# Stationary v for three segments, shared diagonal scores, early split transposes of x, gate operations on GpSimd, and a newly searched order, in a kernel of segmented attention beside a spectral layer

## The chip, the cores and the metric

The kernel runs on one core of one Trainium2 chip. The metric is device time in microseconds (us), the median of several runs. A run also has a span (what the profile covers, 1.7 to 2.1 us shorter than the time of the same run) and a mean granted clock of TensorE (PE below), 1.0 at full speed. ACT is ScalarE, DVE is VectorE, POOL is GpSimd, SP is the engine that issues most transfers.

A ratio below is the mean time of one kernel's fast runs over the mean of the other's fast runs of the same rounds, so it is not quite the ratio of the medians quoted beside it. The interval is the 95% interval of that ratio. "Same" means within 2%. The calls ran on different chips of the same kind, so kernels of different calls are best compared by their ratios to the kernel before of the same call.

## The reference, cut to what matters

Tokens: 2048, width 640, 32 heads of width 20, in 4 segments of 512. Each segment has causal softmax attention inside itself and reads a linear memory that the segments before it have left. A spectral layer runs on the same input, and a gate per token mixes the two.

```python
for s in range(N):                                   # N = 4 segments of L = 512
    logits = einsum('bhqd,bhkd->bhqk', qs, ks) * scale + mask
    p = softmax(logits);  a_dot = einsum('bhqk,bhkd->bhqd', p, vs)
    num = einsum('bhld,bhde->bhle', phi(qs), M)      # phi(t) = t+1 if t > 0 else exp(t)
    den = einsum('bhld,bhd->bhl', phi(qs), z)[..., None] + 1e-06
    outs.append(g * num / den + (1 - g) * a_dot)
    M, z = M + phi(ks)^T vs, z + sum(phi(ks))
a = o @ wo
b = irfft2(rfft2(x) * (w_r + 1j * w_i))
return gate * a + (1 - gate) * b                     # gate = sigmoid(x . gate_w), per token
```

## The kernel before

The kernel is one flat list of instructions: each engine executes its own in a fixed order that a search has found. Heads are handled in 8 groups of 4 per segment. A score unit fills four PSUM banks by matmuls on row tiles, one exponential of up to 128x2048 moves it to SBUF, POOL zeroes the part above the diagonal, and then the product with v (PV) follows. PV keeps the exponentials stationary and streams 21 columns of v (20 and a column of ones, which gives the softmax denominator), 40 matmuls a group:

```python
def pv_group(self, s, g):                            # (cut)
    for i in range(4):                               # block of 128 queries
        for hh in range(4):
            for jj in range(i + 1):                  # block of 128 keys
                # out 128 x 21, stationary: exponentials 128 x 128, moving: v
                return (self.ps(bank, i * 88 + hh * VW, [1, DH + 1]),
                        self.ex.ap(self.exo(s, g) + hh * 1280 + JOFF[jj] + (i - jj) * P, [1, P]),
                        va.ap(jj * H * VW + (4 * g + hh) * VW, [1, DH + 1]), jj == 0, jj == i, {})
    # DVE: denominators times gate, reciprocal, product -> on (128 tokens per partition block)
    ...
    # later: store of on to DRAM, transposed load of it as oT, output projection with wo
```

The order of the loads at the start is one transposed load of three 128-column blocks of x, then one of two.

The softmax here doesn't subtract the row's maximum and nothing guards it: scores larger than these inputs give would overflow.

## Time and profile before

| what | before |
|---|---|
| median time, 4 runs | 246.55 us (246.41 to 250.81) |
| profiled span, granted clock | 244.2 us, 1.0 |
| PE busy, and span less PE busy | 233.1 us, 11.1 us |
| ACT, DVE, POOL busy | 201.6, 198.8, 132.2 us |
| start of the first score exponential on ACT | 13.32 us |
| moved by DMA | 36.71 MB |

The lines behind these numbers are in the prediction. "Span less PE busy" is the time in which PE does nothing.

### The profile page before, as it was taken

What the parts mean: (1) busy time and instruction counts of PE and PEld (TensorE: products, weight loads), DVE (VectorE), ACT (ScalarE), POOL (GpSimd) and SP (SyncE); (2) the same over time, 40 slices, a digit from 0 to 9 for tenths busy, and PEclk for the clock granted to TensorE, in tenths of its full rate; (3) what the DMA queues carried; (4) which work ended last, traced back from release to release, by engine and by line L of the source; (5) the groups of instructions that cost most, each with busy time, mean ns of one, the idle gap of its engine ahead of it and who ended that gap; (6) DMA issues with size and microseconds to landing.
All of it is one profiled execution on the core that took longest, in us unless ns stands there. A gap on an engine that the chain in (4) does not pass through costs nothing.

```text
span 244.2 us, 8905 instructions
## 1 busy us (share of the span) xinstructions
PE 233.1 (95%) x3702; PEld 139.8 (57%) x3702; DVE 198.8 (81%) x534; ACT 201.6 (83%) x204; POOL 132.2 (54%) x200
## 2 busy tenths in 40 slices
PE   7999999999999999999978999999899999999994
PEld 2344575557556457645644475645555667667683
DVE  1489997988999898979999999989999975643643
ACT  2088889999998998999987998888899878798820
POOL 8421861362648484455876385646567656407610
PEclk9999999999999999999999999999999999999999
DMA  7998866696493656756442546313442969586224
GB/s 185 328 358 231 218 172 169 205 182 172 138 192 92 168 128 150 226 164 200 109 104 71 144 137 182 94 59 111 118 100 71 203 144 97 79 123 116 77 62 131
DMA packets 55880, 36.71 MB, mean 150 GB/s; under 512 B 31792, under 2 KB 52128, under 8 KB 55840
## 3 DMA queue, kind: packets, MB, share of 16 engines
q1 hardware_dynamic: 54144, 35.32, 58.4%
q10 hardware_dynamic: 1696, 0.82, 1.2%
q8 instruction: 29, 0.48, 0.8%
q14 instruction: 11, 0.09, 0.1%
HBM read 19.86 MB, written 9.71 MB: 121 GB/s over the span
## 4 chain that ended last, share of the span: by engine, by line
PE 72%; DVE 16%; DMA 5%; ACT 4%; issue 2%; SPq 0%; DVEq 0%
PE psum L498 64%; PE psum L496 8%; DVE Pt L1287 4%; ACT ex L1137 3%; DMA xT<-in_A_x_dram 2%; DMA oT<-o_scr 2%; DVE Cp L509 2%; DVE Yt L1292 1%; DVE qu L509 1%; ACT et L1010 1%; DVE va L1045 1%; DVE Bt L509 1%; DVE on L1172 1%; DVE on L1177 0%; DVE phk L1021 0%
## 5 line engine op out<-in xcount | busy, mean ns | idle before, releaser
L1137 ACT ACTIVATE ex<-psum 128x2048 bf16<-128x2048 f32 x80 | 150.3, 1878 | 15.8 <-PE psum L498 14.8
L1140 POOL TENSOR_SCALAR_AFFINE_SELECT ex<-ex 128x512 bf16<-128x512 bf16 x128 | 81.0, 653 | 70.5 <-ACT ex L1137 66.7
L498 PEld LDWEIGHTS psum<-va,ex 128*128 128x128 bf16 x1280 | 39.0, 96 | 5.8 <-issue 1.3
L498 PE MATMUL psum<-va,ex 128*128 128x21 bf16 x1280 | 41.1, 172 | 0.1
L498 PE MATMUL psum<-xT,wk 128*128 128x512 bf16 (+1 forms) x140 | 33.3, 380 | 0.6 <-DMA xT<-in_A_x_dram 0.6
L498 PE MATMUL psum<-xT,wq 128*128 128x512 bf16 (+1 forms) x135 | 32.2, 380 | 1.2 <-DVE Bt L509 1.2
L498 PE MATMUL psum<-qp,kp 20*128 20x384 bf16 (+3 forms) x512 | 31.7, 301 | 0.7 <-ACT ex L1137 0.2
L498 PE MATMUL psum<-wv,xT 128*128 128x500 bf16 (+1 forms) x160 | 31.9, 300 | 0.2
L1287 DVE TENSOR_TENSOR Pt<-psum,Wt 128x642 bf16<-128x642 f32 x32 | 25.4, 822 | 0.8 <-PE psum L498 0.5
L496 PE MATMUL psum<-wo,oT 128*32 128x320 bf16 x480 | 23.0, 300 | 0.2 <-issue 0.2
L498 PEld LDWEIGHTS psum<-qp,kp 20*128 20x128 bf16 x512 | 9.0, 92 | 18.3 <-ACT ex L1137 9.6
L509 DVE CAST ot<-psum 128x320 bf16<-128x320 f32 x21 | 9.9, 489 | 11.6 <-PE psum L496 8.4
L498 PEld LDWEIGHTS psum<-wv,xT 128*128 128x128 bf16 x160 | 13.3, 97 | 10.0 <-DVE Ac L509 0.8
L498 PE MATMUL psum<-big,Ac 128*128 128x321 bf16 (+2 forms) x96 | 17.9, 256 | 0.8 <-DVE Cp L509 0.4
L1045 DVE TENSOR_TENSOR va<-psum,ebx 128x500 bf16<-128x500 f32 (+1 forms) x32 | 15.2, 484 | 3.5 <-PE psum L498 2.8
L498 PE MATMUL psum<-tt,Yt 128*128 128x256 bf16 (+1 forms) x96 | 17.0, 274 | 0.4 <-DVE qu L509 0.2
L1292 POOL TENSOR_TENSOR Yt<-Pt 128x321 bf16<-128x321 bf16 x18 | 13.4, 757 | 7.2 <-DVE Pt L1287 4.6
L509 DVE CAST qu<-psum 128x512 bf16<-128x512 f32 x20 | 13.6, 686 | 3.4 <-PE psum L498 3.2
L1333 DVE TENSOR_TENSOR G<-eo,psum 128x320 bf16<-128x320 f32 x32 | 14.9, 479 | 1.7 <-PE psum L496 0.9
L498 PEld LDWEIGHTS psum<-xT,wk 128*128 128x128 bf16 (+1 forms) x140 | 9.9, 97 | 10.9 <-issue 2.3
L1177 POOL TENSOR_TENSOR on<-on,mem 128x320 bf16<-128x320 bf16 x16 | 12.8, 806 | 5.8 <-DVE on L1172 5.8
L1172 DVE TENSOR_TENSOR on<-psum,rs 128x320 bf16<-128x320 f32 x32 | 15.3, 481 | 0.6
(85 smaller groups left out, 379.9 us busy)
## 6 DMA issues: line engine op xcount, KB each, us to landing
tt<-tab_tt SPq DMA_DIRECT2D x16, 256.0 KB, 3.3
xsb<-in_A_x_dram SPq DMA_DIRECT2D x8, 320.0 KB
kp<-k_scr SPq DMA_DIRECT2D x28, 80.0 KB
qp<-q_scr SPq DMA_DIRECT2D x28, 80.0 KB
o_scr<-on SPq DMA_DIRECT2D x12, 160.0 KB
out_dram<-ot SPq DMA_DIRECT2D x12, 160.0 KB
q_scr<-qu SPq DMA_DIRECT2D x6, 256.0 KB
k_scr<-qu SPq DMA_DIRECT2D x6, 256.0 KB, 3.9
```

Of the source, the lines that this page charges most:

```text
L496: h = e.matmul(dst, wt, r_, start=st, stop=sp_, **{**kw, "tile_position": (0, q), "skip_group_check": True})
L498: h = e.matmul(o_, l_, r_, start=st, stop=sp_, **kw)
L509: alts["dve"] = (lambda e: e.tensor_copy(dst(), src()), 67 + 1.04 * n, 68.0)
L1010: self.one("act", lambda e: e.activation(et.ap(0, [1, L]), qsl(), ACT.Exp), L, [qb], [b("et", pi_)], late, name="phi_exp")
L1045: self.one("dve", lambda e: e.tensor_tensor(va.ap(i * H * VW + h0 * VW, [VW, nh], [1, DH]), self.ps(bank, 0, [DH, nh], [1, DH]), self.ebx. ...
L1137: self.one("act", lambda e: e.activation(dst(), src(), ACT.Exp, scale=SC), 4 * width, [bank], [self.exb(s, g, j) for g, j in outs], prio - ...
L1140: self.one("pool", lambda e, g=g, j=j: e.affine_select(self.ex.ap(self.exo(s, g) + JOFF[j], [1280, 4], [1, P]), self.ex.ap(self.exo(s, g) ...
L1172: self.one("dve", lambda e, rs=rs, bank=bank, g=g: e.tensor_tensor(on.ap(80 * g, [D, 4], [DH, 4], [1, DH]), self.ps(bank, 0, [88, 4], [VW, ...
L1177: self.either(lambda e, g=g: e.tensor_tensor(on.ap(80 * g, [D, 4], [1, 80]), on.ap(80 * g, [D, 4], [1, 80]), self.mem.ap(80 * g, [D, 4], [ ...
L1287: self.one("dve", lambda e, ri=ri, Pt=Pt, Wt=Wt, bank=bank: e.tensor_tensor(Pt.ap(ri * 322, [644, 2], [1, KD]), self.ps(bank, 0, [0, 2], [ ...
L1292: fn = lambda e, r=r, a0=a0, a1=a1, op=op, Pt=Pt, Yt=Yt: e.tensor_tensor(Yt.ap(r * 322, [1, KD]), Pt.ap(a0 * 322, [1, KD]), Pt.ap(a1 * 322 ...
L1333: self.one("dve", lambda e, q=q, n2=n2, bank=bank, eo=eo: e.tensor_tensor(self.G.ap(n2 * D + 639 * q, [1 - 2 * q, 320]), eo.ap(q, [1, 320] ...
```

## The change

The intent: PE leads, so let it do PV with v stationary (32 columns of v on one of four column tiles, the exponentials streaming), which needs 24 packed matmuls a group for 40 small ones; compute no score twice on the diagonal, so that exponentials get narrower; start earlier; take work off DVE. The core of the diff (cut: tables, buffers, the new order, the layout of tokens that goes with it):

```diff
-        self.xt_load(0, 0.0, 0, 3)
-        self.xt_load(0, 0.01, 3, 2)
+        self.xt_load(0, 0.0, 0, 1)
+        self.xt_load(0, 0.01, 1, 2)
+        self.xt_load(0, 0.02, 3, 2)
 ...
             for g in (2 * pr, 2 * pr + 1):
-                self.pv_group(s, g)
+                if s < 3:
+                    self.pv_flipped(s, g)
+                else:
+                    self.pv_group(s, g)
 ...
+    def pv_flipped(self, s, g):
+        for n_, (jj, o, n, q0) in enumerate(VPIECES):   # 512, 384, 192, 64, 64, 64 columns
+            for hh in range(4):
+                    return (self.ps(bank, q0, [1, n], p0=32 * hh, np_=32), va.ap(jj * H * VW + (4 * g + hh) * VW, [1, 32]),
+                            self.ex.ap(self.exo(s, g) + hh * 1280 + o, [1, n]), n_ == 0, n_ == 5,
+                            {"tile_position": (0, 32 * hh), "skip_group_check": True})
+        # eviction by ACT or DVE, store of the unnormalised result
+    def denominators(self, s):
+        # load of the denominators, reciprocal, times gate, store as r
 ...
+            # output stage: load r and the stored result, oU = oU * r, oU = oU + mT (memory part), then wo
 ...
-                    items.append((th, n / 4.0))      # scores: row tiles 32 x 128
+                    items.append((th, n / 8.0))      # scores: tiles 32 x 64
```

## The prediction

> **What bounds the kernel now.** I read the page first, then the stage table, the chain of waits and the timelines of three short stretches. From the page:
>
> ```profile
> PE 233.1 (95%) x3702; PEld 139.8 (57%) x3702; DVE 198.8 (81%) x534; ACT 201.6 (83%) x204; POOL 132.2 (54%) x200
> ...
> PE 72%; DVE 16%; DMA 5%; ACT 4%; issue 2%; SPq 0%; DVEq 0%
> ...
> L1137 ACT ACTIVATE ex<-psum 128x2048 bf16<-128x2048 f32 x80 | 150.3, 1878 | 15.8 <-PE psum L498 14.8
> L1140 POOL TENSOR_SCALAR_AFFINE_SELECT ex<-ex 128x512 bf16<-128x512 bf16 x128 | 81.0, 653 | 70.5 <-ACT ex L1137 66.7
> L498 PEld LDWEIGHTS psum<-va,ex 128*128 128x128 bf16 x1280 | 39.0, 96 | 5.8 <-issue 1.3
> L498 PE MATMUL psum<-va,ex 128*128 128x21 bf16 x1280 | 41.1, 172 | 0.1
> L1172 DVE TENSOR_TENSOR on<-psum,rs 128x320 bf16<-128x320 f32 x32 | 15.3, 481 | 0.6
> ```
>
> The third to seventh lines give count, busy time and mean duration, then the idle time before. The reader should see three engines close together: PE leads and carries 72% of the chain, ACT and DVE are both above 80%, and GpSimd has 112 us of idle time, of which 66.7 us is waiting for an exponential. PE's 95% contains pipeline latency (a 21-column matmul is shown as 172 ns), so I count its work from the program. All full-array streams together (projections, v, scores, memory, the spectral half and the output projections) are about 392,000 columns. The timeline of the last projections shows 28 matmuls of 320 columns on 32-column tiles taking 1.12 us, and 4 taking 0.31 us, so (1.12-0.31)/24 = 33.8 ns each, or 0.42 ns per column after packing four side by side. That makes 392,000 x 0.417 = 163 us. The price of a PV group and of a change of array mode is in this stretch of PE's timeline (start, length, what):
>
> ```profile
> 206.02 0.40 PE L498 MATMUL psum<-qp,kp 20*128 20x512 bf16 x4
> 206.35 2.17 PE L498 MATMUL psum<-va,ex 128*128 128x21 bf16 x80
> 208.45 0.40 PE L498 MATMUL psum<-qp,kp 20*128 20x256 bf16 x8
> ```
>
> Two PV groups, 80 matmuls, take (2.17-0.15)/80 = 25.3 ns each, so 1.01 us a group and 32 us for 32 groups. The score unit needs 512 x 0.417 = 213 ns of stream but 0.33 us pass until the next work: about 0.1 us is a change of mode. 80 units with a change on either side are about 16 us. With some 4 us of small gaps between matmuls PE's real work is 163+32+16+4 = 215 us, of a window of 234 us between the first useful matmul (7.4 us) and the last (about 241). The roughly 19 us left are stalls. Where they lie shows in the stage table and at the start:
>
> ```profile
> 110.00:130.00 20.00, 18.16 (x265) 10.82 (x261) 19.70 (x46) 17.87 (x20) 14.30 (x22) 1.00 0.50 135
> 150.00:170.00 20.00, 19.98 (x253) 10.98 (x253) 17.91 (x47) 17.58 (x15) 12.36 (x21) 1.00 0.33 91
> 170.00:190.00 20.00, 18.86 (x281) 11.20 (x279) 19.21 (x63) 18.04 (x17) 13.85 (x19) 1.00 0.39 101
> ...
> 1.27 5.96 DMA xT<-in_A_x_dram
> 7.36 19.51 PE psum L498 x179
> ```
>
> Columns of the first three: PE, PEld, DVE, ACT, POOL busy, clock, DMA. At 110 to 130 and 170 to 190 DVE is full and PE is not; at 150 to 170 PE is full. The last two lines, from the chain in order of time, say that PE cannot start before the transposed load of three blocks of x has landed.
>
> [...]units of eight row-tiled matmuls (384 and 128 columns) last as long as units of four with 512, 0.40 us[...].
>
> **The change part by part.**
>
> *PV with v stationary, segments 0 to 2.* 24 of 32 groups replace 40 matmuls of 25.3 ns by 24 packed ones, six pieces of 512, 384, 192, 64, 64 and 64 columns, together 1280: 1280 x 0.417 = 0.53 us plus small gaps, 0.545 us. The saving is 24 x (1.01-0.545) = 11.2 us of PE. In return it is another array mode: one more change per group, 24 x 0.1 = 2.4 us, and the odd v tiles, whose rows are now permuted by column tiles, up to 16 x 0.2 = 3 us if the order does not bunch them. Net PE about -7.
>
> *Shared diagonal scores.* Per pair of groups the five units have widths 512, 512, 512, 512, 256 where they had five times 512. PE: 16 x 256 x 0.417 = -1.7 us. ACT: 598 ns for 512 and 1878 for 2048 elements make 0.833 ns per element and a fixed 171, so 1024 elements take 1.02 us. Segments 0 to 2: 12 x (1.88-1.02) = -10.2; segment 3 has its exponentials split: four pairs each lose 1.88 and gain two of 0.60, and two units each split at +0.17, so 4 x (-0.68+0.34) = -1.4. Sum -11.6 us of ACT. GpSimd pays: four masks a group become seven, three of 512 elements and four of 256. With 634 ns as typical for 512 and an estimated 430 for 256, a group goes from 2.54 to 3.62 us, 32 groups +35 us.
>
> *Normalisation moved.* DVE loses, per flipped group, 168+244+481 = 0.89 us (the denominators, the reciprocal, the multiplication): 24 x 0.89 = -21.4. It is replaced by 24 evictions of 512 columns (598 ns on ACT, 686 on DVE: +15.4 over the two), 15 products of 512 and 8 sums of 640 bf16 elements on DVE or GpSimd (0.45 and 0.55 us on DVE, so 11.2 there, or some 27 on GpSimd), three reciprocals of 128 columns (the 16 and 32 column ones take 244 and 335 ns, so an estimated 0.9 each) with their products, about 4. The memory sums of segments 1 and 2 (16 at 0.43 to 0.81) go. DVE and ACT together: -11.6-21.4+15.4+4+1.4 (eight more gate exponentials) +6 = about -6 us, of 400.
>
> *Round trip.* The unnormalised result goes out in 12 stores of 256 KB and back in 15 loads of 128 KB, in place of 4 of the 12 stores of 160 KB and 4 of the 12 transposed loads. The DMA share is 0.3 to 0.5 where most of it happens; segment 2's falls into 190 to 210, at 0.81. Weights, tables and padded q and k come in fewer, larger transfers[...].
>
> *Start.* The transposed load of three blocks becomes one block and then two; six warm-up matmuls of 0.43 us go. PE should begin real work 1 to 2 us earlier; I take 1.5.
>
> *Gate operations on GpSimd, new order.* Some 1 to 3 us of DVE; the order cannot be costed by hand.
>
> Sum: PE -7-1.7 = about -9, start -1.5, so 244.2-10.5 = 233.7 us of span if stalls stay at 19 us. DVE was the cause in the two stretches above and loses about a tenth of its work there; I take 2 us of stalls back. 231.7 of span, plus the 2.3 us by which the timed median exceeds the span now (246.55-244.2): 234.
>
> **The rivals.** First, GpSimd becomes the bound. 132+35, less 8 for memory sums, plus some of the moved work, is 165 to 180 us, or 70 to 77%. For it: seven dependent masks stand before each PV group[...]. Against it: 70.5 us of idle time ahead of the masks and no 20 us stretch above 72%. It would return half of the gain: 239 to 242. Second, the small tiles cost a floor of 25 ns each. Score matmuls go from 512 to about 1280, PV from 960 to 576; at 25 ns the scores alone would cost about 15 us more and the kernel would end near 246. The eight-tile units speak against it, but no instruction here is as small as 64 columns on 64-column tiles. Third, ACT stays the bound: it does 14 to 15 us of exponentials in each 20 us now, and if it takes most evictions its sum stays near 197 to 201. Then only 3 to 5 us come: 241. Fourth, the round trip of segment 2 delays the outputs at 205 to 215, where the chain now already holds a 5.2 us transposed load: +2 to 4 us. In the other direction, the three engines all fall and the order has been searched anew with other transfer costs: down to 226.
>
> **Range and chances.** 234 us, with 227 to 241.5 holding it 8 times in 10. Faster by over 2% means under 241.6: 0.88. Within 2%, which needs the tile floor or GpSimd to take nearly everything: 0.10. Slower: 0.02, as no added work is on the engine that leads the chain.
>
> **What would show it.** Right: a flipped group of 24 matmuls within 0.55 to 0.65 us on PE's timeline; exponentials at 128x1024 near 1.02 us and ACT's exponential sum near 139; GpSimd at 165 to 180 us with PE's waits for masks still under 5 us; first projection before 6.5 us; DVE below its 19 us of 20 at 110 to 130. Wrong: packed matmuls of 64 columns spaced at 25 ns, PE's loads waiting many us for masks or for ACT, DVE's two-input operations lengthened against the durations above, or a new wait for the returned result between 200 and 220 us.

The sum comes to about -9-1.5 = -10.5, so 233.7 us of span, 231.7 with 2 us of stalls back, and 234 of time. Some of its figures are estimates, and this is what the traces show beside them:

- Its 0.417 ns per column is an estimate; measured are 0.42, both as 33.8 x 4/320 and as three matmuls of 512 columns in 0.65 us (kernel before, 62.18 to 62.83). The 0.15 us taken off two PV groups is about the shown length of one 21-column matmul less its spacing (172 less 25 ns).
- The 0.1 us for a change of mode is an estimate from score units: the next work starts 0.32 to 0.33 us after such a unit does (206.02 to 206.35), where 512 columns on the whole array take 0.215. That the change of mode is the cause was not shown.
- The floor of 25 ns in the second rival is a supposition: the 25.3 ns of the 21-column matmuls carried over to other shapes.
- The estimated 430 ns of a mask of 256 elements were 481 in the changed kernel (128x256, mean of 128). "Some 27" us on GpSimd is an estimate too: a sum of 640 takes 1.39 us there in both kernels, a product of 512 by r 1.16 in the changed one.

## The result, and the profile after

The changed kernel took 247.12 us (246.77 to 247.59, 4 runs) against 246.55 (246.41 to 250.81) of the same rounds. The ratio of the fast runs is 1.0026 (1.0003 to 1.0049): the same within 2%, where 234 was predicted, and outside the predicted range. Executions over 1.5% slower than the fastest of the same kernel are left out of the means. The granted clock was 0.985 to 0.993 in all four runs of the changed kernel.

The page of the changed kernel, in the form of the one before (busy us, share and count of each engine; the chain that ended last by engine; masks; exponentials):

```profile
PE 229.2 (94%) x4347; PEld 141.3 (58%) x4361; DVE 197.3 (81%) x481; ACT 199.3 (81%) x241; POOL 166.5 (68%) x297
...
PE 59%; DVE 14%; DMA 10%; ACT 9%; SPq 3%; issue 2%; ACTq 0%; DVEq 0%
...
L1284 POOL TENSOR_SCALAR_AFFINE_SELECT ex<-ex 128x256 bf16<-128x256 bf16 (+2 forms) x224 | 122.1, 567 | 41.1 <-ACT ex L1263 37.7
...
L1263 ACT ACTIVATE ex<-psum 128x2048 bf16<-128x2048 f32 (+4 forms) x92 | 138.7, 1508 | 13.9 <-PE psum L514 12.0
```

The work moved as planned. Exponentials are 138.7 us where 150.3 were, masks 122.1 where 81.0 were, and POOL stands at 166.5. The DMA engines moved 42.17 MB where they moved 36.71. PE is busy for 3.9 us less, but the span is not shorter: span less PE busy is 244.7-229.2 = 15.5 us, 4.4 more than before. And PE's 229.2 us hold a stretch at half clock, which the stage table shows (columns: PE, PEld, DVE, ACT, POOL busy, granted clock, DMA share, GB/s):

```profile
206.00:208.00 2.00, 1.58 (x58) 1.26 (x42) 1.97 (x5) 1.69 (x2) 1.60 (x2) 1.00 1.11 119
208.00:210.00 2.00, 0.96 (x16) 0.63 (x20) 1.93 (x6) 0.36 (x1) 0.28 (x2) 0.58 0.19 39
210.00:212.00 2.00, 2.00 (x56) 1.00 (x48) 1.11 (x3) 1.11 (x3) 0.80 (x2) 0.50 0.61 163
212.00:214.00 2.00, 2.00 (x40) 0.93 (x36) 0.75 (x2) 0.52 (x1) 1.46 (x3) 0.50 1.34 134
214.00:216.00 2.00, 2.00 (x44) 1.19 (x48) 0.53 (x2) 1.76 (x2) 0.00 (x0) 0.71 0.48 91
```

The lost clock adds up to 2 x (0.42+0.50+0.50+0.29) = 3.4 us, that is 6.8 us at half clock. So PE's work at full clock fell by up to 3.9+3.4 = 7.3 us (a little less, since PE stood idle in a part of that stretch). The reader should see that a busy PE here is partly a slow PE: at 210 to 214 it shows 2.00 of 2.00.

What stopped PE just before is in the timelines of PE, DVE and POOL (start, length, what; in brackets the idle time ahead and what ended it):

```profile
209.04 0.46 PE L514 MATMUL psum<-G,fbg 128*32 128x320 bf16 x4 [1.46 <-DVE on L1325]
```

```profile
206.98 1.60 DVE L1534 TENSOR_TENSOR oU<-oU,mT 128x640 bf16<-128x640 bf16 x1
208.51 0.48 DVE L1325 TENSOR_TENSOR on<-psum,rs 128x320 bf16<-128x320 f32 x1
```

```profile
206.84 1.39 POOL L1534 TENSOR_TENSOR oU<-oU,mT 128x640 bf16<-128x640 bf16 x1 [0.40 <-DVE rs L1320]
```

PE waited for the normalised product of a PV group (L1325), and DVE had put a sum of the new output stage (L1534) ahead of it, which lasted 1.60 us beside the same kind of sum on POOL (the seven such sums of DVE in this trace take 0.43 us at the least and 0.48 in the median). In two later traces it took 1.08 us beside POOL's sum (the late sum moved, at 207.16, and both losses mended, at 205.54), and in all three it ended 0.34 to 0.35 us after POOL's did; what ties the two, no record names. That is one loss of the changed kernel. The other is at the start. The chain there and PE's timeline:

```profile
4.45 6.75 DMA xT<-in_A_x_dram
```

```profile
5.70 1.05 PE L514 MATMUL psum<-xT,wq 128*32 128x512 bf16 x8
...
11.25 0.40 PE L514 MATMUL psum<-xT,wq 128*32 128x512 bf16 x4 [1.70 <-DMA xT<-in_A_x_dram]
```

PE begins at 5.70 instead of 7.36, as predicted, but the third piece of x takes 6.75 us to land, PE stands still for 1.70 us, and the first score exponential starts at 14.83 us, 1.5 later than before.

### The profile page after: what moved, and what is told of

Read it like the earlier page. It is cut to its first block, busy times and chain, and to the rows that moved or that the text cites. A ratio compares the mean times of both kernels' runs of the same rounds, so it can differ in the third digit from the quotient of the medians.

```text
span 244.7 us, 10242 instructions
## 1 busy us (share of the span) xinstructions
PE 229.2 (94%) x4347; PEld 141.3 (58%) x4361; DVE 197.3 (81%) x481; ACT 199.3 (81%) x241; POOL 166.5 (68%) x297
## 2 busy tenths in 40 slices
DMA packets 58928, 42.17 MB, mean 172 GB/s; under 512 B 30020, under 2 KB 55172, under 8 KB 58884
## 4 chain that ended last, share of the span: by engine, by line
PE 59%; DVE 14%; DMA 10%; ACT 9%; SPq 3%; issue 2%; ACTq 0%; DVEq 0%
PE psum L514 53%; PE psum L512 7%; ACT ex L1263 6%; DMA xT<-in_A_x_dram 3%; DMA pkn<-phk 2%; SPq L548 2%; DMA r<-r_scr 2%; DVE Pt L1439 2%; DMA qk_scr<-qu 2%; DMA r_scr<-rc 2%; SPq L546 1%; DVE G L1485 1%; DVE phk L1085 1%; DVE oU L1526 1%; ACT et L1072 1%
## 5 line engine op out<-in xcount | busy, mean ns | idle before, releaser
L1284 POOL TENSOR_SCALAR_AFFINE_SELECT ex<-ex 128x256 bf16<-128x256 bf16 (+2 forms) x224 | 122.1, 567 | 41.1 <-ACT ex L1263 37.7
L1263 ACT ACTIVATE ex<-psum 128x2048 bf16<-128x2048 f32 (+4 forms) x92 | 138.7, 1508 | 13.9 <-PE psum L514 12.0
L514 PE MATMUL psum<-qkp 20*64 20x64 bf16 (+5 forms) x1280 | 32.7, 272 | 2.2 <-ACT ex L1263 1.7
L514 PE MATMUL psum<-xT,wk 128*128 128x256 bf16 (+1 forms) x280 | 34.1, 276 | 0.2 <-issue 0.2
L514 PE MATMUL psum<-wv,xT 128*32 128x321 bf16 (+3 forms) x400 | 30.1, 301 | 0.6 <-DVE va L1115 0.3
L512 PE MATMUL psum<-wo,oU 128*32 128x320 bf16 x480 | 23.5, 319 | 0.0
L514 PE MATMUL psum<-big,Ac 128*128 128x160 bf16 (+2 forms) x96 | 18.1, 258 | 0.7 <-DVE Pt L1439 0.3
L514 PE MATMUL psum<-big,Cp 128*128 128x321 bf16 (+1 forms) x96 | 18.0, 302 | 0.2 <-DVE G L1485 0.2
L514 PE MATMUL psum<-ex,va 128*32 128x64 bf16 (+3 forms) x576 | 17.4, 256 | 0.7 <-DVE dn L1152 0.3
L514 PEld LDWEIGHTS psum<-ex,va 128*32 128x32 bf16 x576 | 11.1, 96 | 9.7 <-POOL ex L1284 3.4
L1072 ACT ACTIVATE et<-qu 128x512 bf16<-128x512 bf16 x25 | 15.6, 629 | 0.1
```

What stands on the lines that cost most here:

```text
L512: h = e.matmul(dst, wt, r_, start=st, stop=sp_, **{**kw, "tile_position": (0, q), "skip_group_check": True})
L514: h = e.matmul(o_, l_, r_, start=st, stop=sp_, **kw)
L1072: self.one("act", lambda e: e.activation(et.ap(0, [1, L]), qsl(), ACT.Exp), L, [qb], [b("et", pi_)], late, name="phi_exp")
L1263: self.one("act", lambda e, d=d, q=q: e.activation(self.ex.ap(*d), self.ps(bank, *q), ACT.Exp, scale=SC), n, [bank], [self.exb(s, 2 * pr + ...
L1284: self.one("pool", lambda e: e.affine_select(self.ex.ap(e0 + d0, [1280, 4], [1, n], np_=np_), self.ex.ap(e0 + s0, [1280, 4], [1, n], np_=np_),
```

## The experiments

Sixteen kernels ran. Each call had its own runs of the kernel before (medians 246.49 to 246.72), except where another is named. "Mended" is the kernel of the fourth run, the changed kernel with both losses above taken out.

### First question: are the start and the late sum what ate the gain?

The theory: the two losses above cost about 4 us together, and the rest of the predicted saving was never there. The rival: the saving is there and some larger thing eats it.

**Start.** The second half of wk (560 KB) and one 320 KB block of x, which the ACT queue issued beside the transposed loads, go to the SP queue behind the third of them. In the list of the order:

```diff
-  ... 35 (wk, second half, ACT queue) ... 45 (x block, ACT queue) ... 30 (third transposed load) ...
+  ... 30 (third transposed load), 34 (wk, SP queue), 44 (x block, SP queue) ...
```

> Changed kernel, only the place of two early loads altered: 560 KB of wk and 320 KB of x go out on the sync queue behind the third transposed piece of x instead of on ACT's queue beside it. Theory (the loads on ACT's queue share the 16 DMA engines with the third transposed piece, which then lands at 11.25 us and holds PE): the third piece lands before 9.6 us, the first score exponential starts near 13 us instead of 14.8, and the time falls by 1.5 to 2 us. Rival (the split into three pieces itself is slow): it still lands near 11 us and the time does not change.

Measured: 243.75 us, ratio 0.9854 (0.978 to 0.9928), result right. Its two runs at full clock took 242.5 and 242.1, two at clock 0.986 took 245.0 and 247.4 (the last counts as slow). That is more than the 1.5 to 2 us expected. The third piece of x is no longer waited for on PE's timeline, and the first exponential starts at 13.70:

```profile
9.63 0.39 PE L514 MATMUL psum<-xT,wq 128*32 128x512 bf16 x4
...
11.99 0.27 PE L514 MATMUL psum<-xT,wk 128*128 128x256 bf16 x1 [0.45 <-DMA wk<-in_A_wk_dram]
```

**The split itself.** The transposed load goes back to three blocks and two, the ACT loads stay.

```diff
-        self.xt_load(0, 0.0, 0, 1)
-        self.xt_load(0, 0.01, 1, 2)
-        self.xt_load(0, 0.02, 3, 2)
+        self.xt_load(0, 0.0, 0, 3)
+        self.xt_load(0, 0.01, 3, 2)
```

> Changed kernel with the two-piece split of the kernel before (three blocks, then two; a 8 KB dummy load keeps the number of operations), the loads on ACT's queue left where they are. Rival of the last run (the split is the cause): PE's first projection waits until about 7.3 us but then runs through, first exponential near 13.3, time down 1.5 us. Theory (competition): the second piece still lands late, first exponential at 14.5 or later, time unchanged or up by up to 1 us.

Measured: 249.99 us, ratio 1.0125 (1.007 to 1.0181), with the first exponential at 16.89 us: worse than either side had expected. The split was not the fault; undone alone it makes things worse, because the wait moves to the second half of wk:

```profile
14.54 1.66 PE L514 MATMUL psum<-xT,wk 128*128 128x256 bf16 x10 [3.25 <-DMA wk<-in_A_wk_dram]
```

**The late sum.** One entry of the order moves: DVE's first sum of the output stage goes behind the product that PE waits for.

```diff
-  ... 4160 (sum oU + mT, DVE), ... 3830 (product on, DVE) ...
+  ... 3830 (product on, DVE), 4160 (sum oU + mT, DVE) ...
```

> Changed kernel, only one DVE operation moved: the memory sum of 640 columns that ran at 206.98 for 1.60 us goes behind the multiplication that frees the PSUM bank PE waits for at 207.6 to 209.0. Theory (this wait idles PE for 1.46 us and the idle PE has its clock halved for the next 6.8 us): PE's gap there shrinks to under 0.5 us, the clock stays 1.0, and the time falls by 3 to 5 us. Rival (the halved clock does not come from this gap): the gap shrinks, the clock still falls to 0.5 for a window, and at most 1.5 us are won.

Measured: 244.01 us, ratio 0.988 (0.9831 to 0.9928), clock 0.992 to 1.0. In its trace the sum starts at 207.16, PE's largest gaps there are 0.15 and 0.54 us, and no slice has half clock.

**Both.**

> The first and the third run together. If both losses are on the path and independent the gains add: 5 to 7 us less than the changed kernel, so 240 to 242 us, 2 to 3% faster than the kernel before. If the kernel is bound by something else meanwhile (GpSimd, ACT, the order of the scores), clearly less than the sum of the two.

Measured: 243.07 us (242.27 to 243.80), ratio 0.9858 (0.9806 to 0.991), result right, clock 1.0 in all four runs. The gains do not add: each alone had brought 3.1 to 3.4 us of the 4.1. A point that all four kernels pass ahead of the late stretch separates the two. PE's first matmuls with wo and oU start at 188.93 us in the changed kernel, 187.17 with the loads moved, 188.46 with the sum moved and 186.98 with both. So the loads are worth about 1.5 to 1.8 us by then, in one trace each, and the rest comes later. The start's two runs at full clock and nearly all runs of the late sum lack the half-clock stretch, so what the two moves have in common is probably this stretch, which either can prevent: with the loads moved alone, the late sum ran at 205.20 for 0.43 us, away from POOL's, and PE's longest gap at 200 to 216 us was 0.53 us. This mended kernel is the best version found, 1.4% faster than the kernel before, which still is "same" by the 2% rule. Its page:

```profile
PE 226.5 (94%) x4347; PEld 140.4 (58%) x4361; DVE 196.9 (82%) x481; ACT 199.4 (83%) x241; POOL 167.0 (70%) x297
...
PE 51%; DVE 19%; ACT 15%; DMA 8%; SPq 3%; issue 2%; DVEq 0%; ACTq 0%
```

PE is busy for 6.6 us less than before at full clock, and the span is only 244.2-240.3 = 3.9 us shorter. Span less PE busy is 13.8 us. So the two losses account for what the change lost against the kernel before, but not for the other 9 us between 243 and 234.

### Second question: why is 6.6 us of PE work worth so little?

**Is POOL the bound after all** (the first rival of the prediction)? The mended kernel with masks a quarter as wide; the result is wrong.

```diff
+        m = 64 if s == 0 and g < 4 else 16
+        n = n * m // 64
-            [[0, 4], [step, n // 64], [1, 64]], ALU.is_ge, ...
+            [[0, 4], [step, n // m], [1, m]], ALU.is_ge, ...
```

> The changed kernel with both losses mended (e4), its masks a quarter as wide after the first four groups (wrong result on purpose): some 60 us less on GpSimd. If GpSimd's masks[...] hold the mended kernel: 3 us or more less than e4's 243.1, DVE's two-input operations shorter. If GpSimd is beside the path: within 1 us of e4.

Measured: 243.28 us, ratio 0.9856 (0.9816 to 0.9896). POOL fell from 167.0 to 123.6 us (43 us, not 60) and DVE from 196.9 to 193.5, and nothing came of it. The two-input operations that DVE's lines of both pages list kept their length (822 and 823, 483 and 483, 483 and 482 ns). For the mended kernel that rival falls.

**Do the changes of array mode eat it?** The mended kernel with the odd tiles of v on the whole array, 14 mode changes fewer (229 to 215 by the count of the program's order, which no trace shows); the result is wrong.

```diff
-  ... for p0, t0, n in ((0, 64, 32), (32, 96, 32), (64, 0, 32), (96, 32, 32)) if i % 2 else ((0, 0, P),):
+  ... for p0, t0, n in ((0, 0, P),):
```

> The mended kernel (e4) with the odd v tiles as one full-array matmul instead of four column tiles (wrong result on purpose), the same order of operations: 14 changes of array mode fewer by the program's order (215 instead of 229). At about 0.1 us each: 1.4 us less than e4. If the changes of mode are hidden: no difference.

Measured: 243.14 us, ratio 0.986 (0.9828 to 0.9893): no difference.

**Removing work from the kernel before.** If PE's time is on the path that sets the end, then leaving out PE work without any other change must shorten the kernel before. The rival is that PE, ACT and DVE are near enough to each other that shortening one uncovers the next. Four runs, results wrong where matmuls or products are left out:

```diff
 # less PV: 288 of 960 PV matmuls of the first three segments left out, 7.3 us of PE by count
+                        if s < 3 and 0 < jj < i:
+                            continue
 # less exponentials: 14 of the shared score units half as wide, 12 us of ACT by count, 10.6 in the trace
+            cut = 2 if s == 0 and pr < 2 else 4
 # less DVE: the spectral product half as wide from the third group on, 9 us of DVE by count, 7.8 in the trace
+                kw = KD if g < 2 else 161
```

> The kernel before, in segments 0 to 2 with 28 instead of 40 PV matmuls a group (wrong result on purpose): 24 x 12 x 25.3 ns = 7.3 us less on PE and nothing else changed, about the net PE saving of the change. Theory of the prediction (PE's work sets the time of the kernel before, saving comes out nearly one to one): 5 to 7 us less, 240 to 241.5. Rival (the order of waits among PE, ACT and DVE sets it; PE's saving turns into waiting): under 2.5 us less, PE's busy time lower but its idle time higher by as much.

> The kernel before, 14 of its 80 exponentials with half their columns (wrong result on purpose): 14 x 0.85 = 12 us less on ACT, about ACT's saving in the change. Theory of the prediction (PE first): 1 to 3 us less. Rival (ACT paces the stretches): 5 us or more less.

> The kernel before with the spectral multiplications of groups 2 to 15 at half width (wrong result on purpose): 28 x 0.33 = 9 us less on DVE. If DVE alone sets the time of the kernel before (it is full at 110 to 130 and 170 to 190 us): 5 us or more less. If PE, ACT and DVE hold it in turn: under 2 us less, as for PE and ACT alone.

> The three cuts together in the kernel before: 7.3 us less on PE, 12 on ACT, 9 on DVE. Theory now (three engines hold each other in turn through a fixed order, none alone): clearly more than the sum of the single ones, 4 to 9 us less. Rival (something else, such as the transfers on the sync queue, holds the pace): under 2 us less even now.

Measured: less PV 247.74 us, ratio 1.0054 (0.9983 to 1.0124); less exponentials 246.44, 1.0035 (0.9968 to 1.0101); less DVE 245.19, 0.9955 (0.9892 to 1.0018); all three 246.32, 0.9963 (0.9884 to 1.0041); its fast runs were 244.87, 244.97 and, at clock 0.993, 247.67. All four intervals include no change. (The check called the result of less exponentials right all the same.) Removing work from all three engines at once seemed to bring nearly nothing. That spoke for a bound outside them, in transfers and the fixed order.

The same on the mended kernel, less DVE:

> The mended kernel (e4, 243.1) with the same cut on DVE (9 us less). If DVE, whose sum the change left where it was, paces the mended kernel: 3 us or more less than e4. If not: within 1 us of e4.

Measured: 243.86 us, ratio 0.9861 (0.9799 to 0.9924): as the mended kernel.

**Adding PE work to the mended kernel.** The first PV piece is computed three times, 10.2 us of PE, result right.

```diff
-        for n_, (jj, o, n, q0) in enumerate(VPIECES):
+        for n_, (jj, o, n, q0) in [(0, VPIECES[0])] * 2 + list(enumerate(VPIECES)):
```

> The mended kernel (e4) with the first piece of each flipped PV group computed three times instead of once, the result unchanged: 24 x 2 x 0.22 = 10 us more on PE, so that PV costs what it did before the change. If PE's time counts one to one: 8 to 11 us more than e4 (251 to 254). If PE's saving was worth a third or less: 1 to 4 us more.

Measured: 254.59 us, ratio 1.0335 (1.0275 to 1.0394), 11.5 us more than the mended kernel, at clocks of 0.987 to 0.998. So PE is on the path when it gets longer, and, if the removal above was a fair test, hardly when it gets shorter.

### Third question: is the removal a fair test?

The removal had brought a loss of its own. Inside a run of eight identical matmuls of the output projection PE stands still, and the trace names no releaser ("issue"). First the kernel before, then less PV (all three looks like it, with 3.42 us):

```profile
209.33 0.44 PE L496 MATMUL psum<-wo,oT 128*32 128x320 bf16 x7
209.93 0.97 PE L496 MATMUL psum<-wo,oT 128*32 128x320 bf16 x21 [0.15 <-issue]
```

```profile
208.71 0.44 PE L496 MATMUL psum<-wo,oT 128*32 128x320 bf16 x7
212.45 0.32 PE L496 MATMUL psum<-wo,oT 128*32 128x320 bf16 x1 [3.31 <-issue]
```

The stall in the two shortened kernels sits 32 matmuls further on in the program than the small gap of the kernel before. The page of the kernel before lists what moves in blocks, among its DMA queues (packets, MB, share of the 16 engines' span):

```profile
q8 instruction: 29, 0.48, 0.8%
```

29 packets of about 16 KB, for 3702 matmuls and 3702 weight loads: one for 255 instructions. The other pages agree on 256: the changed kernel has 34 packets for 4347 matmuls and 4361 weight loads, and of the runs below, one with 512 PE instructions fewer than the kernel before has 27 for its 29, one with 768 more has 32, and one with 768 fewer than the mended kernel has 31 for its 34. So I take a packet for a block of 256 of PE's instructions. The removal took out 288 matmuls with their weight loads, 576 instructions, two blocks and 64 instructions over: exactly the 32 matmuls. So, by this count, these gaps lie at the borders of PE's program blocks. Two kernels remove 256 matmuls instead, whole blocks, so that the border stands where it stood:

```diff
-                        if s < 3 and 0 < jj < i:
+                        if s < 3 and 0 < jj < i and not (s == 2 and i == 2):
```

> The kernel before with 256 of its 960 PV matmuls of the first three segments left out (288 in the run before it): 6.5 us of PE work less, and 512 instructions, two blocks of 256. Displaced fetch: no stall over 1 us without a releaser at 205 to 216 us, granted clock 0.996 or more in most runs, and 242.5 to 244.5 us. True second bound: 245.5 to 247 us as before, whether the stall is there or not.

> The same with 12 us of ACT and 9 us of DVE work left out as well. Displaced fetch: no stall without a releaser, and 240 to 242.5 us. True second bound outside the three engines: 244.5 us or more.

Measured: less PV in whole blocks 245.3 us, ratio 0.9966 (0.9914 to 1.0019). All three in whole blocks 243.28, ratio 0.9876 (0.9831 to 0.9921), clock 1.0 in all runs of both. Both times lie between the two answers, and the first interval includes no change. Of the stall my expectation was half right. The border did go back to its matmul, but in the profiled run of the first there is still a stall at it:

```profile
208.86 0.44 PE L496 MATMUL psum<-wo,oT 128*32 128x320 bf16 x7
211.82 0.97 PE L496 MATMUL psum<-wo,oT 128*32 128x320 bf16 x21 [2.51 <-issue]
```

So the place follows the count of instructions, and the length follows something else. Eight traces side by side, from the queue's timeline and the DMA view in half-microsecond windows (for each: when the last program packet ahead of the border was seen, when a pair of transposed loads of oT was issued and how long that issue lasted, and the stall):

| kernel | program packet | issue of the pair | stall of PE |
|---|---|---|---|
| before | 205.0 | 210.40, 3.63 us | 0.15 us |
| less exponentials | 206.0 | 210.64, 3.25 us | none listed |
| less DVE | 204.5 | 209.49, 3.32 us | 0.20 us |
| all three, whole blocks | 202.0 | 207.38, 3.69 us | none listed |
| less PV | 208.0 | 208.68, 5.33 us | 3.31 us |
| all three | 210.5 | 211.12, 5.42 us | 3.42 us |
| less PV, whole blocks | 209.0 | 209.93, 5.22 us | 2.51 us |
| before, more PV (below) | 217.0 | 217.91, 7.60 us | 4.43 us |

Where the packet came some 5 us ahead of the pair, PE ran on; where it came less than 1 us ahead, PE stood still for 2.5 to 4.4 us and the issue of the pair took 5 us or more. One line of each kind from the queue's timeline, the kernel before and less PV:

```profile
210.40 3.63 SPq L526 DMA_TRANSPOSE oT<-o_scr  x2
```

```profile
208.68 5.33 SPq L526 DMA_TRANSPOSE oT<-o_scr  x2
```

That the transposed loads and the program's fetch hinder each other is argued from these eight traces; no run moved a transposed load to show it.

The stall cannot be what hides the saving, though. All kernels of this family pass one point just ahead of the border: eight score matmuls of 256 columns. In the kernel before it is at 208.45 us (its line is in the prediction). Here it is in less PV in whole blocks, in all three in whole blocks, and in the kernel with more PV of the next test:

```profile
207.98 0.40 PE L498 MATMUL psum<-qp,kp 20*128 20x256 bf16 x8
```

```profile
205.43 0.40 PE L498 MATMUL psum<-qp,kp 20*128 20x256 bf16 x8
```

```profile
215.96 0.40 PE L498 MATMUL psum<-qp,kp 20*128 20x256 bf16 x8
```

Up to this point the granted clock was 1.0 in these traces, and PE had no gap like that of the border. So 6.5 us less PE work had brought 0.5 us by then, the three cuts together 3.0, and 9.4 us more PE work had cost 7.5. The kernels of the first removal agree: less PV 206.74, less exponentials 208.69, less DVE 207.55. These are single traces, and fast runs of the kernel before differ by 1 us and more, so only the size of the numbers counts.

**Removal and addition with whole blocks.** The mended kernel with 384 of its 576 turned PV matmuls left out, 7.0 us of PE (wrong), and the kernel before with 384 PV matmuls done twice (right):

```diff
 # mended, less PV
-        for n_, (jj, o, n, q0) in enumerate(VPIECES):
+        for n_, (jj, o, n, q0) in [(k, p) for k, p in enumerate(VPIECES) if k in (0, 5)]:
 # before, more PV
-                    for jj in range(i + 1):
+                    for rep, jj in ([(1, 0)] if s < 3 else []) + [(0, j) for j in range(i + 1)]:
```

> The mended version (243.1 us) with 384 of its 576 turned PV matmuls left out: 704 columns times 24 groups, 7.0 us of PE work, and 768 instructions, three blocks. If PE sets the pace in this direction too: 236 to 238 us. If half comes out, as the mended version itself kept about half of the saving of the change: 239 to 241. If something else holds it: 242 to 243.5.

> The kernel before with the first PV matmul of each group done twice, 384 more, 9.8 us of PE work and three whole blocks of instructions, right result. If PE is the bound of the kernel before as I had it: 255 to 257 us. If half of its time lies beside other limits: 251 to 253.

Measured, mended less PV: fast runs 241.99, 242.71 and 243.69 us, all at clock 0.993, and two slow ones at 0.986; ratio to the kernel before 0.9821 (0.9788 to 0.9855). The mended kernel had full clock. Giving the 0.7% of clock back (0.007 x 242.7 = 1.7 us) makes 241.0, an estimate, so at most about 2 of the 7 us came out, and 0.4 as measured (242.71 against 243.07, in different calls). As measured this is the third of the answers, with the clock given back the edge of the second. Its page:

```profile
PE 224.5 (92%) x3965; PEld 132.9 (55%) x3977; DVE 196.6 (81%) x481; ACT 199.5 (82%) x241; POOL 166.4 (68%) x297
...
PE 42%; DVE 24%; ACT 15%; DMA 11%; SPq 3%; issue 3%; DVEq 0%
```

This profile is of a slow run, so only its shape counts: PE is down to 42% of the chain, and DVE, ACT and transfers hold half of it. Up to 206 us its clock was full. Its first matmuls with wo and oU start at 187.48 us, against 186.98 in the mended kernel, so nothing had come of the removal by then; a start that was 0.45 us later (first scores at 13.22 for 12.77) hides no more than that.

Measured, before more PV: the two fast runs 253.40 and 253.51 us, ratio 1.0271 (1.0241 to 1.0302); two slow runs at 260.3 and 260.5, whose profile has the 4.43 us stall. A group of 56 matmuls takes 1.55 us on PE's timeline where one of 40 takes 1.16, so the addition was 24 x 0.39 = 9.4 us of PE, and 253.4-246.7 = 6.7 us of it came out.

What the removals and additions say together, in us. PE is counted from the program, except in the last row. ACT and DVE are busy times from the traces. "Time" is the median of the fast runs against the kernel before of the same call; in the three rows "mended, less" and "mended, more" it is against the mended kernel of another call. "At the point" is read from one trace each: the eight score matmuls for the kernel before, the first matmuls with wo and oU for the mended one.

| kernel | PE | ACT | DVE | time | at the point |
|---|---|---|---|---|---|
| before, less PV, whole blocks | -6.5 | | | -1.4 | -0.47 |
| before, less exponentials | | -10.6 | | -0.2 | +0.24 |
| before, less DVE | | | -7.8 | -1.3 | -0.90 |
| before, all three, whole blocks | -6.5 | -11.1 | -6.9 | -3.4 | -3.02 |
| before, more PV | +9.4 | | | +6.7 | +7.51 |
| mended, less PV | -7.0 | | | -0.4 (about -2 with the clock given back) | +0.50 |
| mended, less DVE | | | -7.0 | +0.7 | -0.53 |
| mended, more PV | +10.2 | | | +11.5 (its trace has a 1.82 us stall) | +8.08 |
| mended against before | -6.6 | -2.2 | -1.9 | -3.6 | |

The first three cuts one by one add up to 2.9 us by the time and 1.1 at the point; together they bring 3.4 and 3.0. So "clearly more than the sum", which I had expected of engines that hold each other in turn, shows at the point and not in the timed medians: it is not settled.

## Why the prediction was wrong

*The chain of work was right.* The exponentials' sum (139 predicted, 138.7 measured), POOL's (165 to 180, 166.5), 1024 elements at 1.02 us (1.024 measured), the first projection before 6.5 us (5.70), and waits for masks under 5 us (3.9) all came as written. DVE at 110 to 130 fell below 19 us (18.27). Packed matmuls of 64 columns did not pay a floor of 25 ns each, for 24 of them would then last 0.6 us. A flipped PV group takes 0.73 us on PE's timeline (0.55 to 0.65 predicted; the 0.73 holds the latency of the last matmul, and the next work starts 0.67 us after the group). Both stand in PE's timeline of the changed kernel:

```profile
62.16 0.73 PE L514 MATMUL psum<-ex,va 128*32 128x512 bf16 x24
...
64.89 0.32 PE L514 MATMUL psum<-qkp 20*64 20x64 bf16 x24 [0.19 <-ACT ex L1263]
```

*PE's sum was off by a little.* "Net PE about -7" was itself a rounding the wrong way: the terms before it, -11.2+2.4+3, give -5.8. With the -1.7 of the scores that is -7.5 us; the runs show -6.6 (mended, full clock) to -7.3 (changed kernel, clock given back). Two smaller slips: the 0.417 ns per column is below what its own lines give (33.8 x 4/320 = 0.42), and the 2.3 us from span to time mix two runs, since the profiled run of 244.2 us had taken 245.98.

*The step that failed is the one that turned this into time:* "so 244.2-10.5 = 233.7 us of span if stalls stay at 19 us", and after it "I take 2 us of stalls back". The stalls did not stay. Span less PE busy, which is not the prediction's 19 us but moves with them, went from 11.1 to 15.5 us in the changed kernel and is still 13.8 in the mended one. The prediction had the span fall by 12.5 us, to 231.7: 9 of PE's work and 3.5 of time without it. In the mended kernel it fell by 3.9: 6.6 of PE's work, less 2.7 by which the time without it rose. So of the 8.6 us missing there, 2.4 are PE's sum and 6.2 are stalls. The stage table of the changed kernel shows it in the stretches that the prediction had named:

```profile
110.00:130.00 20.00, 18.14 (x328) 10.48 (x325) 18.27 (x48) 18.09 (x20) 14.79 (x29) 1.00 0.66 184
150.00:170.00 20.00, 18.30 (x328) 10.57 (x334) 17.58 (x41) 19.50 (x23) 15.63 (x29) 1.00 0.40 116
170.00:190.00 20.00, 18.92 (x350) 10.43 (x334) 18.25 (x54) 18.73 (x23) 17.97 (x32) 1.00 0.71 197
```

DVE is no longer full at 110 to 130 and 170 to 190, and PE is as busy there as before (18.14 for 18.16, 18.92 for 18.86); at 150 to 170, where PE was full, it no longer is. (The work in a window is not quite the same in both kernels.)

The runs that removed PE work alone show the exchange: 6.5 us left out of the kernel before bring 1.4 (0.5 at the point ahead of the border), 7.0 left out of the mended one at most about 2. I had read PE's 72% of the chain as a licence to count its saving one to one. It holds nearly so for added work (6.7 of 9.4, 11.5 of 10.2) and not for removed work. My explanation is that ACT and DVE stand at 80% and more and take over the chain as soon as PE lets go; the chain of the mended kernel agrees (PE 51% for 72%, ACT 15% for 4%, DVE 19% for 16%), but this is argued and not shown: less DVE work in the mended kernel brought nothing clear of noise, and all three cuts together only 3.4 us. The prediction's own sum had left ACT and DVE at 394 of 400 us.

*The start went the other way.* "PE should begin real work 1 to 2 us earlier; I take 1.5" is right for the first matmul and wrong for the path. The first score exponential came 1.5 us later, because the loads on the ACT queue shared the DMA engines with the third transposed piece: in its 6.75 us (4.45 to 11.20) the packets of the ACT queue (q10) took 53.9% of the span of the 16 engines, those of the SP queue (q1) 58.5%. Moving them behind it returned the exponential to 13.70.

*The late round trip* was the fourth rival, "+2 to 4 us", and I gave it too little weight. It came. The factors r of the third segment go out and come back on the chain that ended last:

```profile
195.80 4.05 DMA r_scr<-rc
...
199.87 4.66 DMA r<-r_scr
```

What stopped PE, though, was not the wait for the returned result that I had named: a sum of the new output stage stood ahead of PE's product in DVE's order, PE stood still for 1.46 us, and the clock was halved for 6.8 us from within that gap on. That the gap halved it is my reading and not shown alone: the stretch went away with the gap in two runs, but elsewhere a gap of 2.51 us left the clock at 1.0 (less PV, whole blocks), so the length of a gap alone does not say it. Together with the start it cost the change 4.1 us (247.12 to 243.07), which is the whole difference between a tie and 1.4% faster.

*The other rivals.* POOL as the bound: refuted for the mended kernel by the quarter-width masks. The floor of small tiles: refuted by the line above. ACT as the remaining bound, "Then only 3 to 5 us come: 241", was nearest to the mended kernel, but ACT alone does not explain it, as removing 10.6 us of ACT work from the kernel before brought nothing; on the mended kernel that was not tried, so there the rival stands.

*What stays open.* Even with 6.5, 11.1 and 6.9 us removed from three engines only 3.4 us come out. Which of the remaining waits holds the rest, the latency of the transfers' round trips, the fixed order or the dependence of one engine's pieces on another's, no run separates. An obvious rival was not tried: every cut kept the order that a search had found for the durations without it, so a new search might get more out of the same cut. Nor is it shown why PE's next program block comes late in some traces.

## What to carry to other kernels

Before counting an engine's saving as time, test it: leave out that much of its work with a wrong result and see what comes out; and do it in both directions, since here, with three engines over 80%, an addition cost most of itself (6.7 of 9.4 us) and a removal paid a quarter or less (1.4 of 6.5). Compare the traces at a point that all variants pass ahead of any such disturbance. Check also that the shortened program has no new gap of its own, above all PE standing still with no releaser inside a run of equal matmuls. And where a change adds loads or small operations off the critical path, look at what they now stand in front of: moving two loads and one sum was worth 4.1 us here.
